# Memory peaks on VectorE and GpSimd from the third batch, lower weight parts on GpSimd, and a changed order, in a fused attention and mixture-of-experts kernel

## The chip, the cores and the metric

The kernel runs on one core of a Trainium2 chip. The metric is the device time of one execution in microseconds (us). The kernel before takes 404.07 us, the median of three runs (403.71 to 404.66). The core has five engines with a queue of instructions each, which the tables call PE (TensorE, with its weight loader PEld), DVE (VectorE), ACT (ScalarE), POOL (GpSimd) and SP (SyncE, which issues the loads and stores). An engine works through its queue in order, and waits at an instruction until the semaphores that it needs are set.

## What is computed

Attention through 32 memories for each head, and a mixture of eight experts behind it:

```python
# q, k, v: 8 batches, 8 heads, 576 tokens, 64 wide; phi: 8, 8, 576, 32
a = phi - max(phi over tokens);  a = exp(a);  a = a / sum(a over tokens)
k_m = einsum('bhsm,bhsd->bhmd', a, k)
v_m = einsum('bhsm,bhsd->bhmd', a, v)
scores = scale * q @ k_m.T
attn = softmax(scores over the 32 memories)
x = (attn @ v_m), heads side by side               # 4608 tokens x 512
logits = x @ w_gate + modality_bias[modality_id]
e_idx = argmax(logits)                             # one expert for each token
out = prob[e_idx] * (relu(x @ w1[e_idx]) @ w2[e_idx])   # 512 -> 1024 -> 512
```

Everything is float32. The kernel guesses the one expert that all tokens take and computes with it. At the end it counts the tokens that take another one (the "verdict"), and a slow general part runs only if there are any.

## The kernel before

**The mathematics on TensorE.** A float32 product is made of three fast ones: each operand is split into an upper part and the lower rest, and upper times upper, lower times upper and upper times lower are added up in PSUM. In the code the upper parts end in `h` (`xah`, `vwh`, `hh`, `w2h`) and the lower in `l`. `xa` and `xb` are the attention weights of 256 and of 320 tokens of a batch half (parts 0 and 1), by token. Since the output of the attention is only needed multiplied by `w1`, the values `v_m` of each batch are multiplied into `w1` first ("vw", `value_products`), so that the first layer (`hidden`, L588) multiplies weights by `vw`, and the second (`outputs`, L617) the hidden values by `w2`. Both together are most of the work of TensorE: 96 matmuls of L588 and 108 of L617 for a batch.

**The attention of a batch**, step by step, with the tile names of the profile:

- The peak of phi over the tokens. `max` folds the tile `ph` on VectorE in four instructions (L253, L254, L256, L257, tiles `t2top`, `top`). `top` transposes the result on TensorE (L141) and reduces it (L268, `topc`). Then TensorE spreads the peak over the partitions (L278, with `ident`), VectorE subtracts it (L284) and ScalarE takes the exponential (L287, `exp`).
- `sums` folds `exp` in the same way, on GpSimd (tiles `t2sums`, `sums`; on VectorE in the first batch); `kv` multiplies it by k and v (L307) and adds up the sums (L315) in the bank pair 1 of PSUM; VectorE and ScalarE divide (L322 to L334); `kvT` transposes keys and values (L141) and copies them out (L364, L372).
- `vg` (`mem_gate`) multiplies the values by the gate's weights (L391, tiles `wgd`, `vT`). It takes a bank of pair 0, and VectorE copies the result out (L396).
- `scores` (L414) multiplies q, turned on VectorE (L402), by the keys, into both pairs. VectorE transposes the scores out of PSUM, 256 columns of each pair for part 0 and 320 for part 1 (L441), takes maximum (L445) and difference (L447), ScalarE the exponential (L449). These are the steps e00 to e03 and e10 to e13. `normalise` (n00 to n12) sums, divides and turns the weights back (L457 to L473, `aT`), and `a_split` makes the upper part on ScalarE (L482) and the lower on VectorE (L485).
- `logits` (L502) and `gate` choose the expert for each token, `others` counts those that differ, and the verdict sums the counts on TensorE (L543) after the last batch.

**PSUM.** Four banks, the tiles `pe`, go round between vw, the first layer and the second. The bank pairs 0 and 1, the tiles `pair`, serve everything else; there is one buffer of each, so a new tile of a pair waits until all readers of the old one are done.

**The order.** All instructions are placed by a planner, `weave`, at build time: it holds a list of attention steps with due times (in progress of the expert work) and one of expert steps, and a table `TAKES` of what each step takes on each engine. At each point it issues the next attention step if that is ready and due, and otherwise the next expert step. Each engine then runs in this fixed order. The attention of batch b+1 so runs between the matmuls of batch b's experts. In the first batch there is nothing to run beside: `plan_first` writes the order down, with matmuls on a dummy tile `busy` (`warm`, `nothing`; L154, L156) in the gaps, and the weights `w2` of the guessed expert are loaded, split on ScalarE (L647) and GpSimd (L648) beside the first chunks of the first layer.

Of the kernel before, what the change touches and what calls it, by code (L numbers as in the profile page):

```python
# [8 lines left out]
F32 = mybir.dt.float32  # L9
# [4 lines left out]
ALU = mybir.AluOpType  # L14
# [40 lines left out]
def attn_moe(ctx: ExitStack, tc: tile.TileContext, q, k, v, phi, mod_id, w_gate, mod_bias, w1, w2, out):  # L55
# [23 lines left out]
    BUSY = 92, 2  # L79
# [190 lines left out]

    def mem_exp(b):
        ph = phs[b % 2].rearrange("p j (c m) -> p j c m", m=M)
        topc = live["topc", b]
        pe = wk.tile([P, HG, QC * M], F32, name="exp")
        px = pe.rearrange("p j (c m) -> p j c m", m=M)
        pb = bank("mem")
        for g in range(NG):
            nc.tensor.matmul(  # L278
                pb[QP * g:QP * (g + 1), 0:P], lhsT=topc[:, g:g + 1].broadcast_to([P, QP]), rhs=ident,
                start=True, stop=True, tile_position=(0, QP * g),  # L280
            )
        peak = pb[:, 0:P].rearrange("p (j o m) -> p j o m", j=HG, o=1)
# [192 lines left out]
    def a_split(b, part, step=None):  # L475
# [9 lines left out]
        nc.vector.tensor_tensor(l, src, h.bitcast(F32), op=ALU.subtract)  # L485
# [164 lines left out]
    def first_w2(c):  # L650
# [11 lines left out]
        "max": (0.0, "D1.9"), "guess": (0.0, "D0.4"), "top": (0.3, "D0.25"),  # L662
        "exp": (0.35, "D1.5 A0.7"), "first exp": (0.35, "D1.5 A0.7"), "first sums": (0.0, "D1.9"), "sums": (0.0, "P0.5"),
        "vwp": (1.15, ""), "vwu": (0.0, "A1.15"), "vwl": (0.0, "D1.35"),
# [24 lines left out]
    def plan_memory(b, due, floor=0.0):  # L689
        for name, after, what, late in (  # L690
            ("max", [], mem_max, 0.0),
            ("top", [("max", b)], mem_top, 1.5),
            ("exp", [("top", b)], mem_exp, 3.0),
            ("sums", [("exp", b)], mem_sums, 3.2),
            ("kv", [("exp", b), ("sums", b)], mem_kv, 6.0),
            ("kvT", [("kv", b)], mem_turn, 9.0),
            ("vg", [("kvT", b)], mem_gate, 10.4),
# [9 lines left out]
    def plan_first():  # L707
# [16 lines left out]
        add(("top", 0), "top", [("max", 0)], mem_top, 0)  # L724
        add(("guess",), "guess", [], guess)
        nothing(2)
# [11 lines left out]
        nothing(2)  # L738
# [13 lines left out]
        nothing(6, "pe")  # L752
        add(("x", 0, 0), "x0", [("n", 0, 0, 2)], a_split, 0, 0)
# [5 lines left out]
    def plan_steps(b, dues):  # L759
# [47 lines left out]
        if b == B - 1:  # L807
            add(("v",), "verdict", [("others", pair)], verdict)
        for (name, kind, after, what, args), due in zip(todo, dues):
            stage(attention, name, kind, after, what, *args, due=due)  # L810

    def plan_experts(b):
# [21 lines left out]
        for part in range(2):  # L834
            if b == part == 0:

                for terms, kind, lower in ((range(2), "h0a", "vwu"), (range(2, 3), "h0b", "vwl")):
                    for f in range(FCH // 2):
# [5 lines left out]
                        if f % 2 == 0:  # L844
                            second(f // 2 + 2 * last_)
# [241 lines left out]
```

## Time and profile before

| what | value |
|---|---|
| median of the runs | 404.07 us (403.71 to 404.66, three runs) |
| the profiled execution | 405.46 us; its span 403.6 us |
| granted TensorE clock, mean | 0.989 |
| read from HBM, written | 37.29 MB, 18.87 MB |
| busy: PE, DVE, ACT, POOL | 96%, 59%, 36%, 10% of the span |

A row of a timeline gives the start and the duration in us, the engine, the line of the code, the operation, the tile written and those read, the shape, and how many instructions the row joins; in brackets the idle time of the engine ahead of it and what ended it. A row of the waits gives who waited for whom, us in total, how often, and the longest. A piece of the chain gives start, duration, engine, tile, line and number of instructions. Matmuls are pipelined, so the duration of one is longer than the distance to the next.

### The profile page before, as it was taken

What the parts mean: (1) busy time and instruction counts of PE and PEld (TensorE: products, weight loads), DVE (VectorE), ACT (ScalarE), POOL (GpSimd) and SP (SyncE); (2) the same over time, 40 slices, a digit from 0 to 9 for tenths busy, and PEclk for the clock granted to TensorE, in tenths of its full rate; (3) what the DMA queues carried; (4) which work ended last, traced back from release to release, by engine and by line L of the source; (5) the groups of instructions that cost most, each with busy time, mean ns of one, the idle gap of its engine ahead of it and who ended that gap; (6) DMA issues with size and microseconds to landing.
All of it is one profiled execution on the core that took longest, in us unless ns stands there. A gap on an engine that the chain in (4) does not pass through costs nothing.

```text
span 403.6 us, 10100 instructions
## 1 busy us (share of the span) xinstructions
PE 387.7 (96%) x4251; PEld 309.4 (77%) x4254; DVE 238.8 (59%) x581; ACT 143.7 (36%) x342; POOL 39.9 (10%) x79
## 2 busy tenths in 40 slices
PE   5989998999999999999999999999999999989994
PEld 5448885889678878787968879688877879678983
DVE  2677745975697556853686457764488437860400
ACT  1245333524243324332443315343342424341410
POOL 3158010002000200011000200002000200000000
PEclk9799999999999999999999999999999999999998
DMA  6999158634641491518411282524501011341112
GB/s 218 325 384 392 52 155 298 223 130 112 209 172 54 137 317 65 209 35 294 164 26 54 64 317 86 206 82 110 179 17 38 26 29 28 131 159 26 28 28 58
DMA packets 28966, 56.90 MB, mean 141 GB/s; under 512 B 3312, under 2 KB 8432, under 8 KB 28912
## 3 DMA queue, kind: packets, MB, share of 16 engines
q1 hardware_dynamic: 28624, 56.16, 41.8%
q8 instruction: 35, 0.57, 0.6%
q14 instruction: 19, 0.16, 0.1%
q10 hardware_dynamic: 288, 0.01, 0.0%
HBM read 37.29 MB, written 18.87 MB: 139 GB/s over the span
## 4 chain that ended last, share of the span: by engine, by line
PE 90%; DVE 3%; ACT 2%; DMA 2%; issue 1%; POOL 1%; ACTq 0%; POOLq 0%
PE pe L617 50%; PE pe L588 23%; PE pair L307 4%; PE pe L555 4%; PE pair L414 3%; DMA ph<-in_phi_dram 2%; PE pair L502 1%; PE pair L156 1%; PE pair L141 1%; DVE hl L600 1%; ACT exp L287 1%; PE pair L278 1%; PE pe L156 1%; ACT hh L597 1%; PE pair L555 1%
## 5 line engine op out<-in xcount | busy, mean ns | idle before, releaser
L617 PE MATMUL pe<-w2h,hh 128*128 128x512 f32 x288 | 117.9, 409 | 0.4 <-DVE hl L600 0.4
L617 PE MATMUL pe<-w2h,hl 128*128 128x512 f32 x288 | 112.6, 391 | 0.0
L617 PE MATMUL pe<-w2l,hh 128*128 128x512 f32 x288 | 110.4, 391 | 0.0
L600 DVE SCALAR_TENSOR_TENSOR hl<-pe,hh 128x256 fp32r<-128x256 f32 (+2 forms) x160 | 58.6, 393 | 53.7 <-ACT hh L597 53.2
L617 PEld LDWEIGHTS pe<-w2h,hh 128*128 128x128 f32 x288 | 54.0, 188 | 25.4 <-issue 12.9
L597 ACT ACTIVATE hh<-pe 128x256 fp32r<-128x256 f32 (+2 forms) x160 | 53.6, 361 | 39.5 <-PE pe L588 39.0
L617 PEld LDWEIGHTS pe<-w2l,hh 128*128 128x128 f32 x288 | 54.0, 188 | 12.0
L617 PEld LDWEIGHTS pe<-w2h,hl 128*128 128x128 f32 x288 | 54.2, 188 | 9.3
L630 ACT ACTIVATE ob<-pe,gates 128x512 f32<-128x512 f32 x36 | 24.7, 689 | 82.4 <-PE pe L617 43.1
L588 PE MATMUL pe<-xbh,vwh 128*128 128x320 f32 x128 | 39.8, 311 | 0.0
L588 PE MATMUL pe<-xbl,vwh 128*128 128x320 f32 x128 | 39.6, 309 | 0.0
L588 PE MATMUL pe<-xbh,vwl 128*128 128x320 f32 x128 | 39.5, 309 | 0.0
L588 PE MATMUL pe<-xah,vwh 128*128 128x256 f32 x128 | 36.9, 291 | 0.2 <-DVE hl L600 0.2
L588 PE MATMUL pe<-xal,vwh 128*128 128x256 f32 x128 | 35.9, 283 | 0.0
L588 PE MATMUL pe<-xah,vwl 128*128 128x256 f32 x128 | 35.3, 283 | 0.0
L253 POOL TENSOR_TENSOR t2sums<-exp 128x512 f32<-128x512 f32 x7 | 9.0, 1286 | 261.8 <-ACT exp L287 261.8
L588 PEld LDWEIGHTS pe<-xah,vwh 128*128 128x128 f32 x128 | 24.4, 191 | 1.4 <-DVE hl L600 0.7
L588 PEld LDWEIGHTS pe<-xal,vwh 128*128 128x128 f32 x128 | 24.5, 191 | 0.3
L588 PEld LDWEIGHTS pe<-xbh,vwh 128*128 128x128 f32 x128 | 24.1, 188 | 0.5 <-issue 0.2
L588 PEld LDWEIGHTS pe<-xbl,vwh 128*128 128x128 f32 x128 | 24.1, 188 | 0.3
L588 PEld LDWEIGHTS pe<-xah,vwl 128*128 128x128 f32 x128 | 24.0, 191 | 0.3 <-issue 0.3
L588 PEld LDWEIGHTS pe<-xbh,vwl 128*128 128x128 f32 x128 | 24.1, 188 | 0.0
(117 smaller groups left out, 428.7 us busy)
## 6 DMA issues: line engine op xcount, KB each, us to landing
kv_sb<-in_k_dram SPq DMA_DIRECT2D x8, 1152.0 KB, 5.9
kv_sb<-in_v_dram SPq DMA_DIRECT2D x8, 1152.0 KB, 9.4
out_dram<-ob SPq DMA_DIRECT2D x64, 128.0 KB, 2.4
q_sb<-in_q_dram SPq DMA_DIRECT2D x7, 1152.0 KB, 7.3
ph<-in_phi_dram SPq DMA_DIRECT2D x8, 576.0 KB, 4.0
raw<-in_moe_w_dram SPq DMA_DIRECT2D x2, 1024.0 KB, 8.6
raw<-in_moe_w_dram SPq DMA_DIRECT2D x1, 1280.0 KB, 11.0
out_dram<-ob SPq DMA_DIRECT2D x4, 256.0 KB, 2.0
```

Of the source, the lines that this page charges most:

```text
L141: nc.tensor.transpose(dst, src, ident[:rows, :rows])
L156: nc.tensor.matmul(idle, lhsT=busy[:, 0:P], rhs=busy, start=True, stop=True)
L253: eng.tensor_tensor(t2, src[:, :, 0:4 * M], src[:, :, 4 * M:8 * M], op=op)
L278: nc.tensor.matmul(pb[QP * g:QP * (g + 1), 0:P], lhsT=topc[:, g:g + 1].broadcast_to([P, QP]), rhs=ident, start=True, stop=True, tile_posit ...
L307: nc.tensor.matmul(live["kvp"][M * j:M * (j + 1), g], lhsT=pe[half, j, c * M:(c + 1) * M], rhs=kv_sb[half, :, j, c * D:(c + 1) * D], start ...
L414: nc.tensor.matmul(sc[g][M * j:M * (j + 1), a, c0 * BL:(c0 + n) * BL].rearrange("p (c t) -> p c t", t=BL), lhsT=kTs[b % 2][p0:p0 + BL, u, ...
L555: nc.tensor.matmul(pvs[g][M * j:M * (j + 1), :], lhsT=vT[b][rows, j, :], rhs=raw1[rows, j, cols], start=True, stop=True, tile_position=(D ...
L588: nc.tensor.matmul(ph[:, 0:n], lhsT=(vl if k == 2 else vh)[:, g, cols], rhs=xl if k == 1 else xh, start=(g == k == 0), stop=(g == NG - 1 a ...
L597: nc.scalar.activation(hs[0][:, f, h0:h0 + p1 - p0], ph[:, p0:p1], AF.Relu)
L600: nc.vector.scalar_tensor_tensor(hl, ph[:, p0:p1], 0.0, hh.bitcast(F32), op0=ALU.max, op1=ALU.subtract)
L617: nc.tensor.matmul(po, lhsT=tile_columns(hl if n == 1 else hh, f, t), rhs=(w2l if n == 2 else w2h)[:, f, :], start=(f == n == 0), stop=(f ...
L630: nc.scalar.activation(ob, po, AF.Copy, scale=gate_of(b, t))
```

## The change

The diff, cut to what matters:

```diff
-    BUSY = 92, 2
+    BUSY = 92, 9
...
+    def mem_turn_top(b):
+        top = live.pop(("top", b)).rearrange("p j m -> p (j m)")
+        tt = wk.tile([P, HG, BL], F32, name="tt")
+        nc.vector.transpose(tt.rearrange("p j t -> p (j t)"), top)
+        tm = wk.tile([P, HG], F32, name="tm")
+        nc.vector.tensor_reduce(tm, tt, axis=AX.X, op=ALU.max)
+        live["tm"] = tm
+
+    def mem_swap(b):
+        ts_ = wk.tile([P, HG], F32, name="ts")
+        for a in range(HG):
+            o = a ^ 1
+            nc.gpsimd.tensor_copy(ts_[BL * a:BL * (a + 1)], live["tm"][BL * o:BL * (o + 1)])
+        live["ts"] = ts_
+
+    def mem_peak(b):
+        tm = live["tm"]
+        nc.vector.tensor_tensor(tm, tm, live["ts"], op=ALU.max)
+        tb = wk.tile([P, HG, BL], F32, name="tt")
+        nc.vector.tensor_copy(tb, tm.rearrange("p (j o) -> p j o", o=1).broadcast_to([P, HG, BL]))
+        peak = wk.tile([P, HG, BL], F32, name="peaks")
+        nc.vector.transpose(peak.rearrange("p j m -> p (j m)"), tb.rearrange("p j t -> p (j t)"))
+        live["peak", b] = peak
...
     def mem_exp(b):
...
+        if b > 1:
+            peak = live["peak", b].rearrange("p j (o m) -> p j o m", o=1)
+        else:
...
-        nc.vector.tensor_tensor(l, src, h.bitcast(F32), op=ALU.subtract)
+        (nc.gpsimd if b or part else nc.vector).tensor_tensor(l, src, h.bitcast(F32), op=ALU.subtract)
...
-            ("vg", [("kvT", b)], mem_gate, 10.4),
+            ("vg", [("kvT", b)], mem_gate, 14.6 if b > 1 else 21.8),
...
-        nothing(2)
+        nothing(1)
...
-        nothing(2)
...
-        nothing(6, "pe")
-        add(("x", 0, 0), "x0", [("n", 0, 0, 2)], a_split, 0, 0)
+        nothing(2, "pe")
+        add(("xu", 0, 0), "xu0", [("n", 0, 0, 2)], a_split, 0, 0, 0)
+        add(("x", 0, 0), "xl00", [("xu", 0, 0)], a_split, 0, 0, 1)
...
-        if b == B - 1:
-            add(("v",), "verdict", [("others", pair)], verdict)
...
+        if b == B - 1:
+            stage(attention, ("v",), "verdict", [("others", pair)], verdict, due=due + 6.0)
...
-                for terms, kind, lower in ((range(2), "h0a", "vwu"), (range(2, 3), "h0b", "vwl")):
+                for n, (kind, from_) in enumerate((("h0a", ("xu", 0, 0)), ("h0a", ("x", 0, 0)), ("h0b", ("vwl", 0, 0)))):
...
-    AHEAD, SPREAD = 4.0, 0.55
+    AHEAD, SPREAD = (6.0, 9.0), 0.55
...
-    plan_memory(1, 5.9, floor=27.5)
+    plan_memory(1, 1.0, floor=27.5)
```

In words:

- From the third batch on, the peak is spread over the partitions without TensorE: VectorE transposes and reduces (`tt`, `tm`), GpSimd swaps neighbouring groups of 32 partitions in four copies (`ts`), VectorE takes the maximum, copies it wide and transposes it (`peaks`). The exponential's subtraction reads it from SBUF. Batches 0 and 1 keep the old way.
- All lower parts of the weights but the first (15 of 16) are made on GpSimd.
- In the first batch, the first four chunks of the first layer run in three passes: upper weights by upper vw, lower weights by upper vw, upper weights by lower vw. Some of the dummy matmuls go; seven are added at the start of the program.
- Memory work of the second batch is due 4.9 sooner, that of the later ones 2 to 5 sooner, `vg` of all batches later, and the verdict later. The planner's table and its rules for when a step may be picked are changed too.

What this does to the order is seen at three places. **TensorE, third batch.** Before, `vg` (L391, into a tile of pair 0) stands ahead of the scores (L414):

```order
L617 MATMUL pe<-w2h,hh 128x512
L617 MATMUL pe<-w2h,hl 128x512
L617 MATMUL pe<-w2l,hh 128x512
L391 MATMUL pair_1576<-wgd,vT_81 32x16 x4
L414 MATMUL pair_1582<-q_sb_99,kT_77 32x288 x2
L414 MATMUL pair_1583<-q_sb_99,kT_77 32x288 x2
```

Now, with lines numbered 30 higher (L421 is `vg`, L444 the scores, L585 vw, L647 the second layer):

```order
L444 MATMUL pair_1582<-q_sb_99,kT_77 32x288 x2
L444 MATMUL pair_1583<-q_sb_99,kT_77 32x288 x2
L585 MATMUL pe<-raw_104,vT_81 32x512 x8
L647 MATMUL pe<-w2h,hh 128x512
L647 MATMUL pe<-w2h,hl 128x512
L647 MATMUL pe<-w2l,hh 128x512
L647 MATMUL pe<-w2h,hh 128x512
L647 MATMUL pe<-w2h,hl 128x512
L647 MATMUL pe<-w2l,hh 128x512
L421 MATMUL pair_1648<-wgd,vT_81 32x16 x4
L647 MATMUL pe<-w2h,hh 128x512
```

`vg` has moved behind the scores, vw and six matmuls of the second layer, and its tile `pair_1648` takes the place of the scores' `pair_1582` in pair 0. **VectorE, first batch.** Before, the eight lower parts `hl` of the first layer's part 0 are followed by the transposition of part 1:

```order
L600 SCALAR_TENSOR_TENSOR hl<-pe,hh 128x256 x8
L441 STREAM_TRANSPOSE a<-pair_608 128x320
L441 STREAM_TRANSPOSE a<-pair_609 128x320
L445 TENSOR_REDUCE mx<-a 128x20
L447 TENSOR_TENSOR a<-a,mx 128x640
```

Now (L630 is `hl`, L471 the transposition) the four instructions of the second batch's `max` stand between the seventh and the eighth:

```order
L630 SCALAR_TENSOR_TENSOR hl<-pe,hh 128x256 x7
L253 TENSOR_TENSOR t2top<-ph_103 128x512
L254 TENSOR_TENSOR t2top<-t2top 128x4x64
L256 TENSOR_TENSOR top<-t2top 128x128
L257 TENSOR_TENSOR top<-top,ph_103 128x128
L630 SCALAR_TENSOR_TENSOR hl<-pe,hh 128x256
L471 STREAM_TRANSPOSE a<-pair_613 128x320
L471 STREAM_TRANSPOSE a<-pair_614 128x320
```

The eighth `hl` and the whole softmax of part 1 have moved behind `max`. **GpSimd, behind the split of w2.** Before, the sums of one batch are followed by those of the next:

```order
L648 TENSOR_TENSOR w2l<-t2sums,w2h 128x512
L253 TENSOR_TENSOR t2sums<-exp 128x512
L254 TENSOR_TENSOR t2sums<-t2sums 128x4x64
L256 TENSOR_TENSOR sums<-t2sums 128x128
L257 TENSOR_TENSOR sums<-sums,exp 128x128
L253 TENSOR_TENSOR t2sums<-exp 128x512
```

Now (L678 is the split of w2, L515 a lower part of the weights, L285 the swap):

```order
L678 TENSOR_TENSOR w2l<-t2sums,w2h 128x512
L253 TENSOR_TENSOR t2sums<-exp 128x512
L254 TENSOR_TENSOR t2sums<-t2sums 128x4x64
L256 TENSOR_TENSOR sums<-t2sums 128x128
L257 TENSOR_TENSOR sums<-sums,exp 128x128
L515 TENSOR_TENSOR xbl<-aT,xbh 128x640
L515 TENSOR_TENSOR xal<-aT,xah 128x512
L285 COPY ts<-tm 32x4 x4
L515 TENSOR_TENSOR xbl<-aT,xbh 128x640
L253 TENSOR_TENSOR t2sums<-exp 128x512
```

The first batch's `xbl`, the second batch's two lower parts and the third batch's swap now stand in this queue, `xbl` of the first batch behind the sums of the second.

More of the change, by code (lines that the diff above doesn't have):

```diff
@@ L910, in weave @@
             if ra is not None and at[0][3] >= 0 and "D" in TAKES[at[0][1]][1]:
-                ra = max(ra, free["D"] - HOLD[not ex or ex[0][0][0] != "h"])
+                work = sum(float(x[1:]) for x in TAKES[at[0][1]][1].split() if x[0] == "D")
+                ra = max(ra, free["D"] - (HOLD[ex[0][1]] - work if ex and ex[0][1] in HOLD else 3.5))
             if ra is not None and ra <= now and (progress >= at[0][3] or re is None):
@@ L917, in weave @@
             else:
+                assert min(x for x in (ra, re) if x is not None and x > now) < FAR
                 now = min(x for x in (ra, re) if x is not None and x > now)
```

57 lines of the change are left out of this document (33 added, 24 removed), and 4 rows, old and new, of the table TAKES.

## The prediction

> **What bounds the kernel now.** I read the page's busy table first, then the chain that ended last, by engine:
>
> ```profile
> PE 387.7 (96%) x4251; PEld 309.4 (77%) x4254; DVE 238.8 (59%) x581; ACT 143.7 (36%) x342; POOL 39.9 (10%) x79
> PE 90%; DVE 3%; ACT 2%; DMA 2%; issue 1%; POOL 1%; ACTq 0%; POOLq 0%
> ```
>
> TensorE is busy for 387.7 of the 403.6 us span, and 90% of the chain is its own work. So there are two ways to change the time: fewer or cheaper instructions on TensorE, or other waits of TensorE. What VectorE or GpSimd spend counts only where TensorE then waits. The waits of TensorE's matmuls say how little there is to gain:
>
> ```profile
> PE pair L391 <- ACT vT L372: 1.2, 1, 1.2
> PE pair L543 <- DVE bad L541: 1.1, 1, 1.1
> PE pair L414 <- DVE vg L396: 0.6, 2, 0.3
> ...
> PE pe L617 <- DVE hl L600: 0.4, 2, 0.2
> ...
> PE pair L315 <- POOL sums L257: 0.3, 1, 0.3
> PE pe L588 <- DVE hl L600: 0.2, 1, 0.2
> ```
>
> Apart from the start, where inputs arrive, the waits that the change touches add up to 3.8 us. A chain piece of the last batch gives the price of a matmul of the second layer that is not disturbed:
>
> ```profile
> 381.78 16.35 PE pe L617 x72
> ```
>
> That is 16.35 / 72 = 0.227 us each.
>
> **Part 1: the peaks leave TensorE (a gain).** The timeline of TensorE around the peak of one batch, starts in the first column:
>
> ```profile
> 175.74 0.28 PE L588 MATMUL pe<-xah,vwl 128*128 128x256 f32 x1
> 175.86 0.27 PE L141 MATMUL pair<-ident,top 128*128 128x128 f32 x1
> 175.89 0.47 PE L617 MATMUL pe<-w2h,hh 128*128 128x512 f32 x1
> 176.20 0.39 PE L617 MATMUL pe<-w2h,hl 128*128 128x512 f32 x1
> ...
> 177.12 0.40 PE L617 MATMUL pe<-w2l,hh 128*128 128x512 f32 x1
> 177.45 0.44 PE L278 MATMUL pair<-ident,topc 128*64 128x128 f32 x4
> 177.82 0.50 PE L617 MATMUL pe<-w2h,hh 128*128 128x512 f32 x1
> 178.16 0.39 PE L617 MATMUL pe<-w2h,hl 128*128 128x512 f32 x1
> ```
>
> From 177.12 to 178.16 there are two starts of the second layer and one peak: 1.04 instead of 2 x 0.227, so the peak costs 0.58. From 175.89 to 176.20 the first matmul behind the transposition takes 0.31 instead of 0.227, and the transposition itself 0.03: 0.11 together. 0.69 a batch, six batches: **-4.1 us**. The new work lies on VectorE and GpSimd, with 41% and 90% of the span free; what it can cost stands among the rivals.
>
> **Part 2: the waits that go.** The verdict now stands behind other expert work: -1.1. `vg` no longer stands right behind the copies of its own keys and values (-1.2), and scores no longer behind `vg` (-0.6); the sums may start sooner (-0.3): -2.1. The waits for `hl` are 0.6 (0.4 and 0.2): bounds 0 and 0.6, and I take -0.6, since 15 of 16 lower parts, 0.67 each (the row of L485 below), leave VectorE, where `hl` stood behind them. Sum: **-3.8**. Each of these can come back elsewhere, so the lower bound is half, 1.9.
>
> **Part 3: a new wait in five batches (a loss).** `vg` takes a tile of pair 0, and now stands behind the scores that fill pair 0. So it waits until VectorE has transposed part 1 of the scores out of it: two transpositions of part 0, a maximum, a difference, then the first of part 1. Behind the waiting `vg` stand all expert matmuls of TensorE's queue. Whether TensorE waits depends on how much work stands between scores and `vg`. Third batch, TensorE and VectorE of before:
>
> ```profile
> 109.06 1.09 PE L555 MATMUL pe<-raw,vT 64*32 64x512 f32 x16
> ...
> 111.58 0.39 PE L617 MATMUL pe<-w2h,hh 128*128 128x512 f32 x1
> ```
> ```profile
> 112.48 0.91 DVE L441 STREAM_TRANSPOSE a<-pair 128x320 f32<-128x320 f32 x2
> ```
>
> Vw starts at 109.06 behind the scores, and 111.58 is the seventh matmul of the second layer, where `vg` stands now. The first transposition of part 1 ends at 112.48 + 0.46 (half of the pair's 0.91) = 112.94: TensorE waits 1.4. Fourth batch, the scores end at 144.33, in both engines:
>
> ```profile
> 144.33 0.50 PE L617 MATMUL pe<-w2h,hh 128*128 128x512 f32 x1
> ```
> ```profile
> 146.55 0.91 DVE L441 STREAM_TRANSPOSE a<-pair 128x320 f32<-128x320 f32 x2
> ...
> 150.16 0.49 DVE L600 SCALAR_TENSOR_TENSOR hl<-pe,hh 128x320 fp32r<-128x320 f32 x1 [1.85 <-ACT hh L597]
> ```
> ```profile
> 148.54 0.31 PE L588 MATMUL pe<-xbh,vwh 128*128 128x320 f32 x1
> ```
> ```profile
> 148.71 7.05 PE pe L588 x48
> ```
>
> Undisturbed, pair 0 is free 146.55 + 0.46 - 144.33 = 2.68 after the scores. In the fourth batch 18 matmuls of the first layer stand ahead of `vg` (7.05 / 48 = 0.147 each, 2.65 in all: three chunks), and their three `hl` stand ahead of the transposition on VectorE. The third chunk starts 1.76 after the scores, its `hl` 1.62 later (148.54 to 150.16) and takes 0.49, then the transposition 0.46: 4.33. TensorE is there at 2.65: it waits 1.7, and 0.1 more to start, 1.8. In the fifth batch nine matmuls of the second layer stand there (9 x 0.227 + 0.11 = 2.15): 0.5. In the sixth, six (1.47): 1.2. In the seventh and eighth, twelve (2.83): none. The second batch is the longest:
>
> ```profile
> 67.81 1.09 PE L555 MATMUL pe<-raw,vT 64*32 64x512 f32 x16
> 71.79 1.09 PE L555 MATMUL pe<-raw,vT 64*32 64x512 f32 x16
> ```
> ```profile
> 73.86 1.25 DVE L147 TENSOR_TENSOR vwl<-pe,vwh 128x512 fp32r<-128x512 f32 x2
> 75.03 0.67 DVE L485 TENSOR_TENSOR xal<-aT,xah 128x512 fp32r<-128x512 f32 x1
> 75.62 0.90 DVE L441 STREAM_TRANSPOSE a<-pair 128x320 f32<-128x320 f32 x2
> ```
>
> Now six matmuls, vw, twelve matmuls and the second vw stand between scores (end 67.81) and `vg`: 18 x 0.227 + 2 x 1.09 + 0.2 for the changes = 6.5, so TensorE is there at 74.3. The second vw starts 1.47 + 1.09 + 2.72 = 5.3 after the scores, at 73.1; its `vwl` follows 2.07 later (71.79 to 73.86), takes 1.25, and behind it stands the transposition, 0.46: 76.8. The wait is 2.5. Sum: 2.5 + 1.4 + 1.8 + 0.5 + 1.2 = **+7.4**. Bounds: 5.7, if the three `hl` of the fourth batch do not hold up VectorE; 8.0, if each wait also slows the first matmul behind it by 0.11 (177.82 to 178.16 against 0.227).
>
> **Part 4: the first batch.** The first layer needs only the upper weights to start, and dummy matmuls are gone: the lower part's 0.67 and about 0.3 of dummies, 1.0 sooner. But `max` of the second batch now stands on VectorE ahead of the eighth `hl`, while GpSimd splits `w2`:
>
> ```profile
> 29.14 2.54 POOL L648 TENSOR_TENSOR w2l<-raw,w2h 128x512 fp32r<-128x512 f32 x2 [3.77 <-ACT w2h L647]
> ...
> 38.37 1.28 POOL L648 TENSOR_TENSOR w2l<-t2sums,w2h 128x512 fp32r<-128x512 f32 x1
> ```
> ```profile
> 36.42 0.42 DVE L600 SCALAR_TENSOR_TENSOR hl<-pe,hh 128x256 fp32r<-128x256 f32 x1 [0.37 <-ACT hh L597]
> ...
> 38.55 1.79 DVE L447 TENSOR_TENSOR a<-a,mx 128x640 f32<-128x640 f32 x1
> ...
> 48.15 0.66 DVE L253 TENSOR_TENSOR t2top<-ph 128x512 f32<-128x512 f32 x1
> ...
> 49.63 0.29 DVE L257 TENSOR_TENSOR top<-top,ph 128x128 f32<-128x128 f32 x1
> ```
> ```profile
> 150.57 0.82 DVE L447 TENSOR_TENSOR a<-a,mx 128x640 f32<-128x640 f32 x1
> ```
>
> L447, both inputs in SBUF, takes 0.82 with GpSimd idle (150.57), and 1.79 where GpSimd's split had started just before it (38.37 to 39.65, then 0.69 more): 0.97 of waiting. The four instructions of `max` have both inputs in SBUF. Free they take 49.92 - 48.15 = 1.77; I take 0.96 more for each, 5.6. The Trainium skill, page "SBUF — State Buffer", section "Who interferes with whom", says that a VectorE instruction with two SBUF inputs and a GpSimd instruction that reads SBUF shut each other out for a whole instruction, whoever starts first; the row of 1.79 agrees. By that rule each of the four can meet another split, and the last ends at about the same time as by my sum; by the one row alone, only one pays, 0.96 in all, and TensorE would not wait.
>
> The row at 36.42 is the eighth `hl`; the seventh ended 0.37 ahead of it, at 36.05, and so ends at 35.05 now. `max` ends 5.6 later, at 40.65, and the eighth `hl` at 41.1 instead of 36.84: 4.3 late, and so is all that VectorE does behind it, the softmax of part 1 and the logits. TensorE's second layer began at 35.58, and its matmul 15 is the first to need this `hl`: 35.58 + 14 x 0.227 - 1.0 = 37.8, so it waits 3.3 there. What follows is a matter of the rows here:
>
> ```profile
> 35.58 0.40 PE L617 MATMUL pe<-w2h,hh 128*128 128x512 f32 x1
> ```
> ```profile
> 47.99 5.29 PE pe L588 x36
> ```
> ```profile
> 58.38 1.29 POOL L253 TENSOR_TENSOR t2sums<-exp 128x512 f32<-128x512 f32 x1 [18.73 <-ACT exp L287]
> ```
>
> Before, the second part of the first layer began at 47.99. It begins at 47.99 + 4.3 = 52.3, or later by what `xbl` waits on GpSimd behind the second batch's sums (four instructions, the first 1.29): I take 0.6, about half of one. The second batch's peak on TensorE (0.69) is then already done: 4.3 + 0.6 - 0.7 = **+4.2**. Bounds: +3.0, if only three of the four meet a split (-0.96), and +4.8, if `xbl` waits for a whole one; that none does is a rival. The seven dummy matmuls at the start lie ahead of the first input and cost nothing; without that cover they cost 7 x 0.227 = 1.6 at most.
>
> **Sum:** -4.1 - 3.8 + 7.4 + 4.2 = +3.7 us. The profiled execution (405.46, of which 403.6 is the span) goes to 409.2; the median of the runs shown is 1.4 lower, 404.07, and goes to **407.8**.
>
> **The rivals.**
>
> *VectorE is not held up by GpSimd in the first batch.* Only one row shows such a wait, and the splits may be done or be waiting for ScalarE when `max` runs (29.14 has 3.77 idle ahead of it). Then `max` ends at 36.8 and the eighth `hl` at 37.2, before TensorE needs it at 37.8. VectorE's chain is 0.4 later than before, TensorE's 1.0 sooner, and the peak (0.7) is done; `xbl` waits its 0.6 behind the sums: about 0.4 + 0.6 - 0.7 = +0.3 by the first, -1.0 by the second chain; I take -0.2. 407.8 - 4.4 = 403.4. Chance 0.14.
>
> *The wait of `vg` is hidden.* TensorE might run later against VectorE than before, since VectorE has lost the lower parts, so that pair 0 is free in time. For it: five waits of only 0.5 to 2.5. Against it: the distance from scores to pair 0 is set by VectorE's own chain, which starts with the scores. Then part 3 is 0: 400.4. Chance 0.10.
>
> *Both:* 396.0. Chance 0.06.
>
> *GpSimd becomes late for the later batches as well.* Lower parts take 1.29 (the 128x512 row of L253) or more there instead of 0.67, and the swap stands in the same queue; VectorE waits for the swap, with `hl` behind it and TensorE behind those. This ends on the slow side even if the first batch is well. It decides from the point where the swap is later than the `hl` that the order puts ahead of the wait. A lower part of 1.29 that has started in the swap's way holds VectorE for half of that on average, about 0.7, in each of six batches, +4.2: 412.0. For it: sums, lower parts and swap fall into the same stretch. Against: GpSimd is busy for 10% of the span, and the order puts the swap mostly behind idle time. Chance 0.10.
>
> That the change does not do what it says is excluded for TensorE's instructions: the order shows the six peaks gone.
>
> **How the numbers follow.** The forecast keeps 0.60; its own range goes from 404.9 (parts 3 and 4 both at their lower bounds, -1.7 and -1.2) to 410.5 (both at their upper bounds, +0.6 each, and part 2 at three fifths, +1.5). The range goes down to 400.3, to take in the two single rivals; left out are the double rival (0.06) and GpSimd late everywhere (0.10). A difference of 0.2%, 0.8 us, is about what a measurement of this kernel can tell from no change. Faster: half of the first rival (403.4 is 0.7 below the median of before), the second, the double one, and 0.03 of the forecast: 0.07 + 0.10 + 0.06 + 0.03 = 0.26. Same: most of the other half and 0.02 of the forecast: 0.08. Slower: 0.66.
>
> **What would show it.** In the profile after: no L278 behind the second batch, and 0.227 between matmuls there (part 1). TensorE waiting at `vg` for VectorE's transposition out of pair 0 in five batches, 2.5, 1.4, 1.8, 0.5 and 1.2 us (part 3). `max` between 35 and 41 with instructions of 1 to 1.6 us, and a wait of about 3.3 for `hl` in the second layer at 38 (part 4). No wait at the verdict (part 2). The prediction is wrong if TensorE's waits at `vg` are under 3 us in all, or if `max` of the second batch takes under 2.5 us.

## The result, and the profile after

The changed kernel takes 414.58 us (median of four runs, 413.17 to 415.61), the kernel before 403.92 in the same comparison: 1.026 times as long (95% interval 1.022 to 1.030). The forecast was 407.8 with a range up to 410.5: the direction was right, the loss of 3.7 us was 10.7. The profiled execution took 415.61, its span is 413.7, 10.1 more than before. The medians below are over all executions of a kernel; in runs 1, 2 and 6 one execution each was slower (622.03, 411.27 and 405.79 us), and without it the medians are 0.1 to 0.2 us lower.

The page after, the busy table and the chain by engine:

```profile
PE 386.9 (94%) x4221; PEld 309.4 (75%) x4224; DVE 247.2 (60%) x590; ACT 143.0 (35%) x342; POOL 67.0 (16%) x118
PE 81%; DVE 9%; DMA 3%; ACT 2%; POOL 1%; issue 1%; SPq 0%; ACTq 0%; POOLq 0%; DVEq 0%
```

TensorE has thirty instructions fewer and is busy for 0.8 us less, but its own work is 81% of the chain instead of 90%: the new time is waiting. Its waits say where (who for whom, us in total, times, longest):

```profile
PE pair L421 <- DVE a L471: 7.3, 5, 2.5
...
PE pe L647 <- DVE hl L630: 2.0, 1, 2.0
...
PE pe L647 <- issue: 1.1, 1, 1.1
PE pe L618 <- POOL xbl L515: 1.1, 1, 1.1
PE pair L337 <- issue: 0.7, 1, 0.7
...
PE pe L618 <- DVE vwl L147: 0.6, 1, 0.6
```

The first row is the forecast's new wait, `vg` (L421) behind VectorE's transposition out of pair 0: five times, 7.3 us, where 7.4 was forecast. From the timeline the five are 2.5, 1.4, 1.6, 0.5 and 1.2. The second row and the fourth are the first batch. The two rows "issue", waits with no releaser, are new and were in no part of the forecast.

The first batch, on VectorE and on GpSimd:

```profile
34.61 0.42 DVE L630 SCALAR_TENSOR_TENSOR hl<-pe,hh 128x256 fp32r<-128x256 f32 x1 [0.37 <-ACT hh L627]
34.95 0.81 DVE L253 TENSOR_TENSOR t2top<-ph 128x512 f32<-128x512 f32 x1
35.80 1.41 DVE L254 TENSOR_TENSOR t2top<-t2top 128x256 f32<-128x256 f32 x1
37.24 1.26 DVE L256 TENSOR_TENSOR top<-t2top 128x128 f32<-128x128 f32 x1
38.54 1.23 DVE L257 TENSOR_TENSOR top<-top,ph 128x128 f32<-128x128 f32 x1
39.69 0.41 DVE L630 SCALAR_TENSOR_TENSOR hl<-pe,hh 128x256 fp32r<-128x256 f32 x1
```
```profile
35.15 3.21 POOL L678 TENSOR_TENSOR w2l<-ob,w2h 128x512 fp32r<-128x512 f32 x2
38.31 1.31 POOL L678 TENSOR_TENSOR w2l<-t2sums,w2h 128x512 fp32r<-128x512 f32 x1
```
```profile
37.77 0.39 PE L647 MATMUL pe<-w2h,hh 128*128 128x512 f32 x1
40.16 0.50 PE L647 MATMUL pe<-w2h,hl 128*128 128x512 f32 x1 [2.00 <-DVE hl L630]
```

The four instructions of `max`, 0.66, 0.42, 0.29 and 0.29 before, take 0.81, 1.41, 1.26 and 1.23, and GpSimd's pair 3.21 instead of 2.55: they take turns. From 34.95 to 39.77 it is 4.8, where the forecast had 5.6, and TensorE waits 2.0 for the eighth `hl`, where it had 3.3. The matmul that waits is the sixteenth of the second layer, not the fifteenth as the forecast read it, which is 0.23 of the difference.

What the forecast did not have stands in a table by stretches. The columns are the stretch, its length, the busy time of PE, PEld, DVE, ACT and POOL, each with its number of instructions, the granted TensorE clock, the share of the DMA engines and GB/s. First behind the wait for `hl`, then behind the second batch's wait at `vg` (76.15 to 78.62):

```profile
42.00:43.00 1.00, 1.00 (x4) 0.81 (x3) 0.84 (x2) 0.33 (x1) 0.00 (x0) 0.50 0.00 0
43.00:44.00 1.00, 1.00 (x4) 0.71 (x4) 0.00 (x0) 0.41 (x1) 0.00 (x0) 0.50 0.00 0
...
79.00:80.00 1.00, 1.00 (x4) 0.80 (x4) 0.96 (x3) 0.00 (x0) 0.19 (x1) 0.69 0.98 397
80.00:81.00 1.00, 1.00 (x4) 0.81 (x3) 0.71 (x1) 0.00 (x0) 0.00 (x0) 0.50 0.96 385
81.00:82.00 1.00, 1.00 (x4) 0.71 (x4) 0.00 (x0) 0.00 (x0) 0.00 (x0) 0.50 0.35 139
```

The clock is halved for 3.4 us in each case (41.82 to 45.24 and 79.37 to 82.78), beginning 1.7 and 0.8 us after TensorE has gone on. The matmuls start 0.427 apart instead of 0.227: six of them, 1.2 us, in the first place, and eight, 1.6 us, in the second. And the two "issue" waits, inside and behind the products of keys and values (L337) of the third and fourth batches:

```profile
104.48 2.15 PE L337 MATMUL pair<-kv_sb,exp 64*32 64x128 f32 x131
107.29 0.33 PE L337 MATMUL pair<-kv_sb,exp 64*32 64x128 f32 x7 [0.66 <-issue]
...
150.65 0.50 PE L647 MATMUL pe<-w2h,hh 128*128 128x512 f32 x1
152.24 0.40 PE L647 MATMUL pe<-w2h,hl 128*128 128x512 f32 x1 [1.09 <-issue]
```

From start to start they cost 0.9 and 1.4 us. TensorE waits for nothing that another engine makes there.

### The profile page after: what moved, and what is told of

The parts are those of the page before. It is cut to its first block, busy times and chain, and to the rows that moved or that the text cites. A ratio compares the mean times of both kernels' runs of the same rounds, so it can differ in the third digit from the quotient of the medians.

```text
span 413.7 us, 10120 instructions
## 1 busy us (share of the span) xinstructions
PE 386.9 (94%) x4221; PEld 309.4 (75%) x4224; DVE 247.2 (60%) x590; ACT 143.0 (35%) x342; POOL 67.0 (16%) x118
## 4 chain that ended last, share of the span: by engine, by line
PE 81%; DVE 9%; DMA 3%; ACT 2%; POOL 1%; issue 1%; SPq 0%; ACTq 0%; POOLq 0%; DVEq 0%
PE pe L647 44%; PE pe L618 24%; PE pair L337 3%; PE pair L444 3%; DMA kv_sb<-in_v_dram 3%; PE pe L585 2%; PE pair L532 1%; DVE a L471 1%; DVE vwl L147 1%; PE pair L141 1%; DVE lg L542 1%; POOL t2sums L253 1%; DVE a L477 1%; DVE mx L475 1%; DVE a L497 1%
## 5 line engine op out<-in xcount | busy, mean ns | idle before, releaser
L647 PE MATMUL pe<-w2h,hh 128*128 128x512 f32 x288 | 118.4, 411 | 0.0
L647 PE MATMUL pe<-w2h,hl 128*128 128x512 f32 x288 | 114.1, 396 | 3.1 <-DVE hl L630 2.0
L647 PE MATMUL pe<-w2l,hh 128*128 128x512 f32 x288 | 111.1, 394 | 0.0
L630 DVE SCALAR_TENSOR_TENSOR hl<-pe,hh 128x256 fp32r<-128x256 f32 (+2 forms) x160 | 59.2, 393 | 56.7 <-ACT hh L627 55.6
L647 PEld LDWEIGHTS pe<-w2h,hh 128*128 128x128 f32 x288 | 55.0, 191 | 23.7 <-issue 11.7
L647 PEld LDWEIGHTS pe<-w2h,hl 128*128 128x128 f32 x288 | 55.0, 191 | 12.3 <-DVE hl L630 2.4
L647 PEld LDWEIGHTS pe<-w2l,hh 128*128 128x128 f32 x288 | 54.3, 189 | 13.3 <-issue 1.3
L618 PE MATMUL pe<-xah,vwh 128*128 128x256 f32 x128 | 35.7, 287 | 0.6 <-DVE vwl L147 0.6
L515 POOL TENSOR_TENSOR xal<-aT,xah 128x512 fp32r<-128x512 f32 x7 | 9.1, 1302 | 156.7 <-ACT xah L512 156.7
L471 DVE STREAM_TRANSPOSE a<-pair 128x256 f32<-128x256 f32 (+1 forms) x32 | 13.6, 460 | 19.6 <-PE pair L444 19.6
L147 DVE TENSOR_TENSOR vwl<-pe,vwh 128x512 fp32r<-128x512 f32 x28 | 17.9, 682 | 12.0 <-ACT vwh L146 12.0
```

Of the source, the lines that this page charges most:

```text
L471: nc.vector.transpose(a[:, g].rearrange("p a c m -> p a (c m)"), sc[g][:, :, RA * part * BL:(RA * part + n) * BL])
L515: (nc.gpsimd if b or part else nc.vector).tensor_tensor(l, src, h.bitcast(F32), op=ALU.subtract)
L618: nc.tensor.matmul(ph[:, 0:n], lhsT=(vl if k == 2 else vh)[:, g, cols], rhs=xl if k == 1 else xh, start=(g == k == 0), stop=(g == NG - 1 a ...
L630: nc.vector.scalar_tensor_tensor(hl, ph[:, p0:p1], 0.0, hh.bitcast(F32), op0=ALU.max, op1=ALU.subtract)
L647: nc.tensor.matmul(po, lhsT=tile_columns(hl if n == 1 else hh, f, t), rhs=(w2l if n == 2 else w2h)[:, f, :], start=(f == n == 0), stop=(f ...
```

## The experiments

Times are medians; the ratio is to the kernel before on the same chip, with its 95% interval. "The changed kernel" is 414.58, 1.026 (1.022 to 1.030).

**1. vg early.** In the changed kernel:

```diff
-            ("vg", [("kvT", b)], mem_gate, 14.6 if b > 1 else 21.8),
+            ("vg", [("kvT", b)], mem_gate, 10.4),
```

> The changed kernel with one number undone: vg is due at 10.4 again for all batches, so that it stands ahead of the scores; nothing else is moved but vg and the scores by a few matmuls. Theory (the wait of vg for pair 0 is a loss of its own): the five waits of 7.3 us go, with them the half clock of 1.6 us behind the 2.5 us wait of the second batch, and a wait of at most 1.5 us for the copies of keys and values comes back in some batches: 414.6 - 7.3 - 1.6 + 1.5 = about 407. Rival (TensorE only waits there because it is ahead of VectorE, and waits elsewhere if not there): 412 to 414, with new waits for hl or for transpositions.

405.7 us, 1.003 (0.999 to 1.006): 8.9 us come back (10.0 between the profiled spans). No wait at `vg` for a transposition is left and no half clock at 79 to 83, the fourth batch's stall is 0.5 from start to start instead of 1.4, and what returns is the wait of the scores for `vg`, in this run's waits:

```profile
PE pair L444 <- DVE vg L426: 0.9, 3, 0.3
```

The theory holds and the rival falls: TensorE does not wait elsewhere instead.

**2. The second batch's memory later.** In the changed kernel:

```diff
-    plan_memory(1, 1.0, floor=27.5)
+    plan_memory(1, 2.2, floor=27.5)
```

> The changed kernel with the second batch's memory work due 1.2 later (2.2 instead of 1.0): max then stands behind the difference of the first batch's part 1 on VectorE, behind the eighth hl, and the first batch's xbl stands ahead of the second batch's sums on GpSimd. Theory (max behind GpSimd's splits holds up the eighth hl): the wait of 2.0 us for hl, the half clock behind it (1.2 us) and the wait for xbl (1.1 us) go: 414.6 - 4.3 = about 410, in the first 56 us of the span. Rival (the first batch is bound by VectorE's total work before the logits, wherever max stands): within 1 us of 414.6.

408.3 us, 1.008 (1.005 to 1.011): 6.3 less, more than expected, since `vg` of the second batch now stands behind six matmuls of the next first layer as well and its 2.5 us wait went too (four waits at `vg`, 4.8 us, are left). The wait for `hl` is gone. `max` still meets GpSimd's last split, but behind the `hl`:

```profile
37.53 1.77 DVE L253 TENSOR_TENSOR t2top<-ph 128x512 f32<-128x512 f32 x1
39.34 0.43 DVE L254 TENSOR_TENSOR t2top<-t2top 128x256 f32<-128x256 f32 x1
```

A new wait of 1.9 us for output tiles (`ob`) takes part of it back, with 3.4 us of half clock behind it (50.46 to 53.87).

**3. Lower parts back on VectorE.** In the changed kernel, TensorE's order untouched:

```diff
-        (nc.gpsimd if b or part else nc.vector).tensor_tensor(l, src, h.bitcast(F32), op=ALU.subtract)
+        nc.vector.tensor_tensor(l, src, h.bitcast(F32), op=ALU.subtract)
```

> The changed kernel with all lower parts of the weights on VectorE again; TensorE's order stays. Theory (the lower parts on GpSimd gain the waits for hl of 0.6 us and cost the wait for xbl of 1.1 us): 414 to 416, the xbl wait gone, the waits at vg longer by up to 0.7 us in the batch where a lower part stands ahead of the transposition. Rival (GpSimd late for later batches is what costs the unexplained part): about 410.

418.01 us, 1.033 (1.030 to 1.037): 3.4 slower than the changed kernel, against both. GpSimd is not what makes the change slow; without it VectorE reaches pair 0 later still (second batch 3.1 instead of 2.5) and the weights for the logits too:

```profile
PE pair L421 <- DVE a L471: 7.8, 5, 3.1
...
PE pair L532 <- DVE aT L503: 1.4, 4, 0.4
```

The wait of 3.1 us is followed by 6.8 us of half clock (77.98 to 84.81) instead of 3.4.

**4. Lower parts on GpSimd, in the kernel before** (the same line the other way).

> The kernel before with another part alone: 15 of the 16 lower parts of the weights on GpSimd, TensorE's order as before. Theory (what the forecast said): the waits for hl of 0.6 us go, and at most one of 0.6 for xbl comes: 403.5 to 404.1. Rival (from the run with all of them back on VectorE, which was 3.4 us slower than the changed kernel: VectorE is late in more places than the waits of before show): 401 to 402.

404.41 us, 1.000 (0.998 to 1.001). There the edit is worth nothing: the three waits for `hl` stay. So its worth in the changed kernel comes from the changed order, the half clock of run 3 included.

**5. The second batch's wait filled.** In the changed kernel, ahead of the stage of `vg`:

```diff
+            if name == "vg" and b == 1:
+                stage(attention, ("fill", b), "nothing", [], warm, 11, False, "pe", due=due + late)
```

> The changed kernel with eleven dummy matmuls (11 x 0.227 = 2.5 us, a product that nobody reads) on TensorE right ahead of the second batch's vg, where it waits 2.5 us. Theory (the half clock after that wait comes from the idle time itself): the clock stays at 1.0 between 79 and 83 us and the time falls by about 1.6 us, to 413.0. Rival (the clock falls for another reason, such as the load of the chip or where the program is): half clock there as before, 414.6 or a little more.

413.14 us, 1.023 (1.020 to 1.026): 1.4 less than the changed kernel, though the intervals overlap. The clock is plainer. The same stretches as above:

```profile
79.00:80.00 1.00, 1.00 (x6) 0.83 (x5) 0.18 (x1) 0.00 (x0) 0.00 (x0) 1.00 0.84 328
80.00:81.00 1.00, 1.00 (x10) 0.96 (x9) 0.00 (x0) 0.61 (x1) 0.00 (x0) 1.00 0.07 20
81.00:82.00 1.00, 1.00 (x11) 1.00 (x10) 0.42 (x1) 0.96 (x3) 0.00 (x0) 1.00 0.00 0
```

With TensorE busy through the wait, the clock stays at 1.00: the idle time halves it. The load of the DMA engines is no reason, since it was 0.00 where the clock was halved at 42 to 44. In this execution the clock stayed whole behind the first batch's 2.0 us wait, too, where nothing was filled; in the other six profiles with that wait it was halved. The traces tell why: their record of the granted clock changes only at steps of 3.41 us. Here are the steps around that wait, with the columns of above, in the changed kernel (37.77 to 40.16 from start to start) and in this run (37.71 to 40.10):

```profile
38.41:41.82 3.41, 1.34 (x5) 0.92 (x6) 3.31 (x7) 0.00 (x0) 1.21 (x1) 1.00 0.62 230
41.82:45.24 3.42, 3.42 (x18) 2.23 (x16) 1.02 (x2) 0.74 (x1) 0.00 (x0) 0.50 0.00 1
```
```profile
35.84:39.25 3.41, 2.25 (x10) 1.52 (x9) 3.34 (x3) 0.00 (x0) 3.41 (x3) 1.00 1.06 393
39.25:42.66 3.41, 2.24 (x9) 1.67 (x10) 3.34 (x7) 0.05 (x1) 0.31 (x1) 1.00 0.36 134
```

In the changed kernel one step holds most of the idle time, 3.41 - 1.34 = 2.1 us, and the next step has half clock. Here a step ends at 39.25, in the middle of the wait, each side gets 1.2 us, and the clock stays whole. In all seventeen profiles, from 25 us on and up to 8 us ahead of the end, the 13 steps at whole clock with 1.87 to 2.98 us of idle time were each followed by half clock (one step of it, twice two), and no step with 1.82 us or less was; nearer to the start and the end, steps with up to 2.0 us passed without it. So by these profiles the idle time within one step decides, with the edge at 1.8 to 2.0 us, and a wait of about 2 us halves the clock or not by where the steps fall in that execution.

**6. Both undone (1 and 2), and what is left.**

> The changed kernel with both undone: vg due at 10.4, and the second batch's memory 1.2 later. Theory (the two losses lie in different places and add up): vg alone undone gave 405.7, and the first batch's stalls there are 2.2 (hl), 1.2 (half clock), 1.1 (xbl) and 0.5 (output tiles), 5.0 in all, of which the other kernel took a wait of 1.9 for output tiles and 1.0 of half clock in their place: about 401.5 to 403, below the kernel before. Rival (the first batch is only moved): 405 to 406.

401.85 us, 0.993 (0.990 to 0.995): below the kernel before, so the two losses lie in different places and add up. Then the gates were put ahead of the second batch's exponential:

```diff
-            ("exp0" if b < 2 else "exp", [(peaks[-1][0], b)], mem_exp, 3.0 if b > 1 else 1.5),
-            ("sums", [("exp0" if b < 2 else "exp", b)], mem_sums, 3.2 if b > 1 else 1.5),
+            ("exp0" if b < 2 else "exp", [(peaks[-1][0], b)], mem_exp, 3.0),
+            ("sums", [("exp0" if b < 2 else "exp", b)], mem_sums, 3.2),
```

> The changed kernel with vg due at 10.4, the second batch's memory 1.2 later, and the exponential and the sums of the first two batches due 1.5 and 1.7 later, so that VectorE makes the first batch's gates ahead of the second batch's exponential. Theory (the wait of 1.9 us for output tiles at 47.6, seen without this last edit, comes from the gates standing behind the exponential's 1.4 us): that wait goes and with it the half clock, 401.85 - 2 = about 400. Rival (the output tiles wait for ScalarE's own work): 401.9.

401.8 us, 0.994 (0.992 to 0.996): no gain, the theory falls. The wait for `ob` is 1.7, and ScalarE's row tells why: the gates are done at 48.1, but the exponential still stands ahead of `ob` in ScalarE's queue and waits for VectorE's difference.

```profile
48.87 1.26 ACT L317 ACTIVATE exp<-exp 128x640 f32<-128x640 f32 x2 [1.44 <-DVE exp L314]
50.03 1.24 ACT L660 ACTIVATE ob<-pe,gates 128x512 f32<-128x512 f32 x2
```

A version that also has the loads of phi later (7), and holds this exponential back behind the first layer:

```diff
-            stage(attention, (name, b), name, after, what, b, due=due + late, floor=floor if name in ("max", "kv") else 0.0)
+            stage(attention, (name, b), name, after, what, b, due=due + late, floor=floor if name in ("max", "kv") else 44.8 if (name, b) == ("exp0", 1) else 0.0)
```

> As the run at 400.3 (vg sooner, second batch's memory 1.2 later, phi's loads behind the products), with the second batch's exponential held back behind the first batch's last chunks of the first layer, so that ScalarE makes the first output tiles ahead of it. Theory (the wait of 1.7 us for output tiles comes from ScalarE's order, the exponential standing ahead of them): that wait goes: 398.6 to 399. Rival (the second batch's keys and values are then late, one behind the other): 401 or more.

405.92 us, 1.004 (1.003 to 1.006). The wait for `ob` goes (0.4 from start to start is left), and TensorE waits 2.4 and 1.0 us for the second batch's weights instead, with half clock behind them (79.30 to 82.71): a loss, as the rival said.

**7. Instructions that come late.** Four runs. The loads of phi behind the products of keys and values, first on the version with `vg` early, then on the last but one version of 6, then on the changed kernel itself:

```diff
-        if b > 1 and b + 2 < B:
-            load_phi(b + 2)
...
     def mem_kv(b):
         kv_products(b)
         kv_divide(b)
         more_keys(b)
+        if b > 1 and b + 2 < B:
+            load_phi(b + 2)
```

> The changed kernel with vg due at 10.4 and the loads of phi issued behind the products of keys and values instead of behind the sums; TensorE's order is that of the run with vg alone undone (405.7). Theory (TensorE's stalls without a releaser beside these products, 1.0 us in the third batch and up to 1.6 in the fourth, are its instructions arriving late behind phi and the output stores on the DMA queues): the stall of the third batch goes, 405.7 - 1.0 = 404.7. Rival (they hang on the place in the instruction stream alone): the stall is there at the same matmul, and 405.7 stays.

405.14 us, 1.001 (0.999 to 1.003), against 405.7: not to be told apart in time; the stall in the third batch is 0.4 instead of 1.0.

> The run beside it, with the loads of phi also issued behind the products of keys and values. Theory (instructions of TensorE late behind other DMA traffic): the stall of the third batch halves, 0.5 to 0.9 us less than the run beside it. Rival: no difference.

400.32 us, 0.991 (0.989 to 0.993), against 401.8: the stall is 0.2 instead of 0.8. This is the fastest version tried.

> The changed kernel with the loads of phi issued behind the products of keys and values; TensorE's order is kept. Theory (TensorE's instructions come late behind other DMA traffic, which the forecast left out): the stall of 0.9 us in the third batch shrinks to 0.2 to 0.5, and the time by 0.5 to 1.0: about 413.7. Rival (the stall hangs on the place in the stream alone): 414.6 and the stall stays.

412.95 us, 1.022 (1.020 to 1.024): the third batch's stall is gone, the fourth's is 1.5 and stays.

Then the place in the stream was moved, by twenty small dummies fewer at the start (`BUSY = 72, 9` on the version at 401.8), and by the seven of the diff (`BUSY = 92, 2` on the changed kernel):

> As the first of these runs, with twenty of the small dummy matmuls at the start of the program left out, so that every later instruction of TensorE stands 40 places sooner; the dummies lie ahead of the first input. Theory (the stalls without a releaser are late instructions, which come in pieces of the stream): the stalls in the products of the third and fourth batch stand at another matmul, 20 further on, or are gone, and the time moves by up to 1.5 us either way. Rival (they come from a port or a bank that these products share): the same matmul, the same length.

408.18 us, 1.010 (1.008 to 1.013): 6.4 us slower for leaving out work ahead of the first input. Without and with the edit, the products of the third batch:

```profile
96.00 2.15 PE L337 MATMUL pair<-kv_sb,exp 64*32 64x128 f32 x131
98.69 0.34 PE L337 MATMUL pair<-kv_sb,exp 64*32 64x128 f32 x7 [0.54 <-issue]
```
```profile
19.46 0.47 PE L337 MATMUL pair<-kv_sb,exp 64*32 64x128 f32 x8 [4.73 <-issue]
...
102.41 2.25 PE L337 MATMUL pair<-kv_sb,exp 64*32 64x128 f32 x144
104.40 0.21 PE L345 MATMUL pair<-ones_c,sums 64*32 64x1 f32 x7
106.26 0.24 PE L345 MATMUL pair<-ones_c,sums 64*32 64x1 f32 x9 [1.60 <-issue]
```

The stall in the third batch stands behind 131 products and sums there and behind 151 here, exactly twenty further on; the fourth batch's stall has gone, the second batch has one of 0.9 us, and the first batch's products, while k and v are still arriving, have one of 4.7 us, with half clock from 18.73 to 28.97 behind it.

> The changed kernel with the seven dummy matmuls at the start left out again, fourteen places of TensorE's instruction stream. Theory of the forecast (they lie ahead of the first input and cost or gain nothing): 414.6. Rival (they set where in the stream the products of keys and values lie, and an instruction piece that comes late there costs up to 5 us, as leaving out forty places did): a stall without a releaser in the first batch's products, 2 to 5 us, 417 to 420.

412.63 us, 1.021 (1.017 to 1.024): if anything faster than the changed kernel (the intervals overlap), against both. The third batch's stall is 1.6 from start to start instead of 0.9, the fourth's 1.4 has gone, and none came in the first batch.

```profile
106.74 0.31 PE L337 MATMUL pair<-kv_sb,exp 64*32 64x128 f32 x3 [1.29 <-issue]
```

Counted from the start of the program, the stalls of over 0.6 us beside these products stand at TensorE's matmul 221, 726, 1236 to 1240 and 1742 to 1748 in all kernels that have them: some 510 apart, one in the products of each of the first four batches. The kernel before passes these places without one; its third batch's products also hold matmul 1236, but hardly a transfer runs beside them (DMA share 0.04 from 100 to 104).

The traces also hold the instructions on their way. The page of the changed kernel lists this DMA queue (packets, MB, share of 16 engines):

```profile
q8 instruction: 35, 0.57, 0.6%
```

These are 35 packets of 16,384 bytes, one for about 241 of TensorE's 8445 matmuls and weight loads (no other engine has over 600 instructions). In the changed kernel such packets land at 105.89 and 150.88, and TensorE goes on from its two stalls at 107.29 and 152.24, 1.4 us later. With twenty dummies fewer one lands at 18.07, and TensorE goes on at 19.46. From 12 us on the profiles have 24 stalls of TensorE without a releaser with 0.3 us of idle time or more, and in each TensorE goes on 1.2 to 1.5 us after a packet of this queue has landed. So these stalls come from late instructions, not from a port or a bank. With the loads of phi later, the third batch's packet begins when TensorE is at matmul 1101 instead of 1137, and the fourth's at 1675 instead of 1676: that is why only the third batch's stall went.

**8. The peaks alone, in the kernel before.** The three new functions, the exponential's new input and the stages for them from the third batch, with the old due times; then with all attention of these batches due 1.0 sooner.

```diff
+            ("ttop", [("max", b)], mem_turn_top, 0.8),
+            ("swap", [("ttop", b)], mem_swap, 1.0),
+            ("top", [("swap", b)], mem_peak, 2.0),
...
-    AHEAD, SPREAD = 4.0, 0.55
+    AHEAD, SPREAD = 5.0, 0.55
```

> The kernel before with one part of the change: from the third batch the peaks on VectorE and GpSimd, in the same place of the plan. Theory (each peak costs TensorE 0.69 us and the new work is hidden): 404.1 - 4.1 = 400.0. Rival (VectorE waits for GpSimd's swap with hl behind it, 0.7 for each batch): 404.

409.89 us, 1.014 (1.011 to 1.016).

> The kernel before with the peaks of the third to eighth batch on VectorE and GpSimd, and all attention work of these batches due 1.0 sooner, so that the third batch's keys and values are not left for the end. Theory (each peak costs 0.69 us of TensorE, and the 409.9 of the run with the same dues as before came from the third batch's steps standing one behind the other): 404.1 - 4.1 = about 400, up to 402 with a wait or two for sums. Rival (GpSimd and VectorE cannot give the peak in time): 405 or more, with waits of the products for ScalarE's exponential in most batches.

403.01 us, 0.998 (0.996 to 0.999). In the first, the third batch's steps stand one behind the other on TensorE with nothing between them, as its timeline shows, each waiting for the last, and the clock is halved behind them (0.50 from 110 to 114):

```profile
102.94 2.25 PE L337 MATMUL pair<-kv_sb,exp 64*32 64x128 f32 x144 [0.87 <-ACT exp L317]
106.74 0.27 PE L345 MATMUL pair<-ones_c,sums 64*32 64x1 f32 x16 [1.55 <-POOL sums L257]
108.66 0.69 PE L141 MATMUL pair<-ident,keys 128*128 128x128 f32 x2 [1.65 <-ACT values L362]
```

In the second, that is gone, and of 4.1 us that the peaks cost 1.0 is gained. Against the waits of before, those for `hl` have grown from 0.6 to 1.7 and those for sums from 0.3 to 1.0:

```profile
PE pe L618 <- DVE hl L630: 1.7, 2, 0.9
...
PE pair L345 <- POOL sums L257: 1.0, 3, 0.5
```

## Why the prediction was wrong, step by step

- **Part 1, the peaks, -4.1.** TensorE's instructions went as forecast. "The new work lies on VectorE and GpSimd" with most of the span free was too quick: alone, the edit gains 1.0, and only with other due times. It makes the way to the sums longer, and the products wait. In the changed kernel the sums of the seventh and eighth batches hold up TensorE by 0.4 and 0.5 from start to start.
- **Part 2, the waits that go, -3.8.** The verdict's, the copies' and `hl`'s waits of before went. A wait for `vwl` of 0.6 came. The lower parts on GpSimd bring nothing in the old order (run 4) and 3.4 in the new one (run 3), half clock included, which no row of before could show.
- **Part 3, `vg`, +7.4.** Right in mechanism, place and size: 7.3, batch by batch. But the step priced a wait at its length. Undoing it gave 8.9, though 0.9 of waits came back, since the 2.5 us wait also halves the clock behind it (run 5), 1.6 us in the profile, and a stall of the supply of instructions shrank by 0.9 with it. That these add up to 8.9 exactly is chance: the interval of the run is 1.5 us to either side. (The forecast's own figures for the second batch, 76.9 less 74.3, give 2.6, not 2.5.)
- **Part 4, the first batch, +4.2.** The taking of turns between `max` and GpSimd is there (4.8 against 5.6). The wait for `hl` was 2.0, not 3.3; but 1.2 of half clock follow it, and `xbl` cost 1.1 instead of 0.6. The second part of the first layer begins at 52.0 instead of 47.99 and waits another 1.1 for `xbl` and 0.3 for output tiles: 5.4 late, less the peak's 0.7 already done, 4.7. Without the half clock that is 3.5. So that 4.7 lies close to the forecast's 4.2, and under its bound of 4.8, is luck: the wait was too long in the forecast, and the half clock was missing. (The lower bound, 4.2 - 0.96, is 3.2, not 3.0.)
- **The step that failed is the sum itself:** it held only lengths of waits, and put what follows a wait, and TensorE's supply of instructions, at nothing without a reason. The half clock, 2.8 us in the two places, and late instructions, 2.3, were left out. "The seven dummy matmuls [...] cost nothing" missed that instructions ahead of the first input move the places of the stream: seven fewer made no loss here (412.6), twenty fewer cost 6.4. With these 5.1, -0.7 in part 4, 0.9 for sums and 0.6 for `vwl`, the forecast of +3.7 becomes +9.6, beside 10.1 between the spans and 10.7 between the medians. The last 0.5 is not assigned, and how much of the late instructions each transfer accounts for was not separated beyond the loads of phi.
- **The rivals.** None of them came. GpSimd blocking VectorE was real, the wait of `vg` was not hidden, and no lower part stood in the swap's way: VectorE waited in five batches, 3.5 us in all and 1.0 at most, but for the swap itself (0.84 us): GpSimd had been idle ahead of it every time, and TensorE had no wait for `hl` there.

## What to carry to other kernels

Where a step takes a bank, look for who reads the bank's last tile, and count the work between: that gave the largest loss to 0.1 us. Then price a wait of TensorE of about 2 us or more with the half clock that can follow it, here 1.2 to 1.6 us on top. And before a part of an order is judged, try it in the order where it will stand: the same edit was worth 0 and 3.4 us.

## What the runs showed of the hardware that was not expected

- **The clock after a wait.** The granted clock changes at steps of 3.41 us, and away from the start and the end of the program a step with 1.87 us or more of idle time on TensorE was always followed by half clock, a step with up to 1.82 never (run 5). So waits of 2.5 us halved it each time, the wait of 2.0 us in six profiles of seven, one of 1.9 in one profile (run 2) and not in another (the first of 6), and waits of 1.4 and 1.6 did not. The Trainium skill, page "TensorE: Matmul & The Clock Gate", section "Why this matters for your kernels", asks for no idle gap above about 3 us; here 2.0 was enough. The same page, section "What's actually happening", says that the window that is watched runs freely; the steps of the traces agree, since the wait of 2.0 us lies within one step in the changed kernel and across two in run 5.
- **The supply of instructions.** Stalls with no releaser, with 0.3 to 4.7 us of idle time, each end 1.2 to 1.5 us after a packet of 16,384 bytes of the instruction queue has landed. The Trainium skill, page "Runtime: NRT & Kernel Launch", section "Instruction fetch mechanics", says that instructions are fetched in blocks of 256 while the block before is executed, and that this is mostly hidden. In these runs it is hidden among the long matmuls of the experts and in the products of the fifth to eighth batches; in and right behind those of the first four, where 144 matmuls take 2.25 us, it is not always.
- **VectorE and GpSimd take turns by whole instructions.** Three folds in a row of 0.42, 0.29 and 0.29 us take 1.2 to 1.4 when GpSimd splits beside them, and GpSimd's 1.28 becomes 1.6.
